# A long convolution by FFT in front of a token-mixing MLP: second forward stage in eight 64x32 tiles, first stage in units of four rows and half of the frequencies, shuffled as 448 KB to 16 partitions

## The chip, the core and the metric

The kernel runs on one core of one Trainium2 chip. The metric is device time in microseconds, the median of several executions. The engines that matter here are TensorE (PE; PEld is its weight load), VectorE (DVE), ScalarE (ACT), GpSimd (POOL) and SyncE (SP). GpSimd and SyncE also issue the DMAs that move data between partitions.

## The reference, cut to what matters

Everything has sequence length S = 2048 and D = 448 channels.

```python
def _A_ref(q, k, v, shift_k, ssm_k, ssm_D):
    # k_shift: causal convolution of k with 4 taps per channel
    for t in range(ks):
        k_shift = k_shift + k_pad[:, t:t + S, :] * shift_k[:, ks - 1 - t][None, None, :]
    kv = k_shift * v
    # causal convolution of kv with ssm_k (2048 taps per channel), by an FFT of length 2 S
    kv_f = rfft(kv padded to 2 S); kf_f = rfft(ssm_k padded to 2 S)
    y = irfft(kv_f * kf_f)[:, :S]
    y = y + kv * ssm_D[None, None, :]
    return q * y

def _B_ref(x, w1, b1, w2, b2):
    u = gelu(einsum("bsd,sf->bdf", layernorm(x), w1) + b1)      # F = 1792
    return transpose(einsum("bdf,fs->bds", u, w2) + b2)

h  = x + _A_ref(layernorm(x), k, v, shift_k, ssm_k, ssm_D)      # x is A_q
h2 = h + _B_ref(layernorm(h), w1, b1, w2, b2)
```

## The kernel before, in words

The FFT is written as matmuls with small tables, in two stages. It is done twice forward: for the filter ssm_k (tag "k", tensors KT and TK, steps k1 and k2) and for the product kv (tag "u", tensors V and TU, steps u1 and u2). A sequence position is 16 q + r, with q on 128 partitions and r = 0 to 15 in the free dimension.

**First stage** (`emit_stage1`, matmuls in L1040). For every r a table `E` (two variants x, 128 frequencies each) is multiplied with the data of row r. The matmuls are 128 x 32 column tiles: four rows r stand in the four column tiles, so four matmuls can run side by side. The loop takes four rows (`i`, four times) and in them a quarter of the frequencies (`jh`, four times). Such a group has eight matmuls into a pair of PSUM banks, and one eviction of 128 x 896 to a ring buffer `GR_`: by a copy on ScalarE or VectorE (L1050), or for the first four rows of k by a VectorE addition (L1048), which adds ssm_D on the way. There are 16 groups for each tag. The ring has four buffers of all four quarters (`gring`).

**Shuffle** (L1056). The second stage needs all 16 rows of a frequency together, so after every second group (a pair of quarters) three DMAs scatter the ring buffer to partitions in steps of four of T (TK or TU): two of 112 KB to 8 partitions each from POOL, one of 224 KB to 16 partitions from SP. A pair of quarters lands in half of T's 16 columns: columns with j mod 4 = 0 or 1 from the first pair, 2 or 3 from the second. T has the shape [16 columns, 2, 448] on 128 partitions.

**Second stage** (`emit_stage2`, matmuls in L1075). For each pair of columns `jj` (eight of them) and each half h there are four matmuls with the block table `FW`, 128 rows by 64 columns, two column tiles side by side; then one eviction of 128 x 896 for each h back into T (L719 to L723; for k with a scale, L720 on ScalarE and L723 on VectorE).

**Products and first inverse stage** (`emit_products_i1`). VectorE multiplies TU with TK (L1108), eight matmuls in 64 x 128 row tiles apply the inverse table (L1120), the result is evicted into TU (L719 or L722), and DMAs from POOL and SP scatter it to TZ (L1144; L1133 for the last columns). The second inverse stage (L1240) and the MLP (L1365, L1375, L1387) follow. The loads of w1 and w2 (L1338, L1342, L1349) are issued on SP once the last POOL scatter is done; the load of q (L896) waits for all shuffles of u.

**The convolution of k** with four taps (`emit_kv`) is done by transposes (L947), matmuls in 64 x 128 row tiles (L973) and a VectorE multiplication with v (L988). The first stage of u needs its output. The transposes of ssm_k (L1019), which the first stage of k needs, come before. `emit_tables` makes E, FW and the inverse tables from iotas on POOL (L773 to L787), VectorE integer operations (L803 to L847) and sines on ScalarE (L828, L843); `fields` holds the bit fields that are cut from the partition number. L1006 are matmuls without use that keep TensorE busy at the start.

**What sets the order.** Every operation is recorded with its reads and writes, and a list scheduler (`_Sched.schedule`) puts them in order at build time. Each step of a tag has a rank in the list `WHEN`; among the operations that are ready in the scheduler's own model, an engine takes the one with the lowest rank. `WHERE` says for each eviction whether ScalarE ("a"), VectorE ("d") or whichever is free ("f") takes it. Each engine then works through its list in order and waits where data are not there yet. PSUM has eight banks in four pairs; a group of first or second stage holds a pair until it is evicted.

Of the kernel before, what the change touches and what calls it, by code (L numbers as in the profile page):

```python
# [7 lines left out]
ALU = mybir.AluOpType  # L8
# [4 lines left out]
    "dummy": (283,),  # L13
    "tables": (138, 234, 288, 20, 81, 325, 139, 217,),
    "loads": (91, 107, 134, 143, 231, 216, 80, 297, 0, 238, 183, 285, 228, 299, 145,),
    "kv": (290, 148, 151, 174, 63, 282, 100, 192, 205, 47, 18, 112, 141, 45, 207, 160, 233,),
    "kT": (201, 13, 14, 175, 200, 130, 54, 53,),
    "k1": (132, 135, 152, 226, 122, 144, 165, 213, 68, 51, 154, 167, 89, 168, 262, 336,),
    "k2": (23, 150, 83, 97, 224, 227, 140, 153, 258, 248, 180, 195, 169, 219, 338, 235,),
    "u1": (71, 86, 116, 123, 46, 82, 176, 221, 117, 215, 261, 316, 173, 184, 277, 278,),  # L20
    "xload": (156, 298, 314, 302,),
    "bias": (75, 171,),
    "q": (271, 208, 318, 93, 268, 185, 279, 280, 264,),
    "u2": (133, 142, 220, 210, 241, 249, 64, 114, 159, 196, 137, 189, 1, 115, 252, 251,),
    "i1": (179, 121, 99, 3, 190, 96, 186, 149, 188, 240, 203, 202, 128, 92, 212, 95,),
    "ct": (36, 187, 87, 300,),
    "xn": (257, 17, 6, 222, 161, 317,),
    "w1a": (329, 239, 230, 55,),
    "w1b": (306,),
    "warm": (291, 307, 265, 27, 292, 147, 330, 320, 5, 304, 270, 38, 19, 315, 284, 62, 333, 327, 105, 118, 191, 295,  # L30
        324, 259, 56, 8, 332, 113, 236, 273, 206, 198, 182, 274,),
    "i2": (260, 69, 103, 39, 15, 31, 293, 28, 108, 242, 90, 84, 88, 331, 22, 197, 204, 33, 110, 237, 164, 323, 256,
        310, 73, 214, 223, 170, 44, 79, 157, 177, 16, 211, 328, 281, 131, 250, 4, 247, 158, 294, 109, 40, 29, 104,
        34, 243, 267, 129, 98, 287, 70, 178, 67, 162, 246, 120, 155, 2, 125, 11, 229, 42, 253, 272, 59, 124, 119,
        266, 12, 78, 194, 276, 127, 41, 313, 10, 102, 61, 255, 21, 37, 66, 24, 232, 199, 321, 312, 76, 308, 296, 52,
        111, 303, 163, 319, 58, 65, 339, 209, 26, 326, 337, 289, 85,),
    "w2": (146,),
    "mlp": (218, 57, 136, 126, 77, 30, 25, 48, 60, 9, 305, 72, 166, 245, 301, 172, 50, 181, 418, 419, 420, 421, 422,
        423, 424, 425, 426, 427, 428, 429, 430, 431, 432, 433, 434, 435, 436, 437, 438, 439,),
}  # L40
WHERE = {
    "kv": "ddaffffa",
    "kT": "fadfdddd",
    "k1": "fafaafaffaff",
    "k2": "dfdffadaafdafada",
    "u1": "fffaafadaaddafaa",
    "bias": "a",
    "u2": "fdaafafaaaaadafa",
    "i1": "affadfaaffdaffaf",
    "ct": "ffda",  # L50
    "xn": "aaff",
    "i2": "aaffaadafddf",
# [518 lines left out]
def _build(nc, A_q, A_k, A_v, A_shift_k, A_ssm_k, A_ssm_D, B_w1, B_b1, B_w2, B_b2, out):  # L571
# [5 lines left out]
    Bsz, S, D = A_q.shape  # L577
    F = B_w1.shape[1]
    assert Bsz == 1 and S == 2048 and D == 448 and F == 1792 and A_shift_k.shape[-1] == 4
    R = 16  # L580
    NFC = F // 128
    EPS = 1e-5
    DB = 2 * D
# [42 lines left out]
    with ctx:  # L626
# [47 lines left out]
        o_GR = (o_WR, o_WR + 8 * DB, o_X, o_X + 8 * DB)  # L674

        def GR_(s):
            return view(o_GR[s], [R // 4, 2, D])
# [13 lines left out]
        gring = _Pool(4)  # L691
# [36 lines left out]
        def emit_tables():  # L728
# [44 lines left out]
            op("pool", lambda e, W: e.iota(pc[:, 0:1], [[0, 1]], base=0, channel_multiplier=128), w=[(o_p, 4)])  # L773
            op("pool", lambda e, W: e.iota(gcol, [[0, 8], [512, 16]], base=0, channel_multiplier=0), w=[(o_gc, 512)],
               n=128, est=190.0)
            op("pool", lambda e, W: e.iota(chi, [[0, 2], [1, 4], [0, 16]], base=0, channel_multiplier=0),
               w=[(o_gc + 512, 512)], n=128, est=190.0)
            for a, b_, c_ in ((0, 112, 14), (112, 128, 2)):
                op("pool", lambda e, W, a=a, b_=b_, c_=c_: e.iota(gcm[:, a:b_], [[0, 8], [512, c_]], base=512 * 14 * (a > 0),
                                                                 channel_multiplier=0),  # L780
                   w=[(o_gc + 1536 + 4 * NB, 512, "gm")], n=128, est=190.0)
                op("pool", lambda e, W, a=a, b_=b_, c_=c_: e.iota(chm[:, a:b_], [[0, 2], [1, 4], [0, c_]], base=0,
                                                                 channel_multiplier=0),
                   w=[(o_gc + 2048 + 4 * NB, 512, "cm")], n=128, est=190.0)
            for k, (b0, st_) in enumerate(((2048, -2048), (2048, 2048), (0, 2048))):
                for a, b_ in (((0, 128),) if k == 0 else ((0, 112), (112, 128))):
                    op("pool", lambda e, W, k=k, b0=b0, st_=st_, a=a, b_=b_: e.iota(  # L787
                        cph[:, 128 * k + a:128 * k + b_], [[st_, 2], [0, (b_ - a) // 2]], base=b0, channel_multiplier=0),
                       w=[(o_gc + 1536 + 512 * k, 512, "cp%d" % k)], n=128, est=190.0)
# [7 lines left out]
            fields = ((5, 12), (0, 2048), (9, 3), (7, 15), (7, 15), (11, 3), (13, 1), (11, 2))  # L797
            o_fd = small(64)
            fd = view(o_fd, [16], i32)
            for i, (sh, mk) in enumerate(fields):  # L800
                op("pool", lambda e, W, i=i, sh=sh: e.memset(fd[:, i:i + 1], sh), w=[(o_fd + 4 * i, 4)], est=34.0)
                op("pool", lambda e, W, i=i, mk=mk: e.memset(fd[:, 8 + i:9 + i], mk), w=[(o_fd + 32 + 4 * i, 4)], est=34.0)
            op("dve", lambda e, W: e.tensor_tensor(out=pc[:, 4:12], in0=pc[:, 0:1].broadcast_to([128, 8]), in1=fd[:, 0:8],  # L803
                                                   op=ALU.logical_shift_right),
               r=[(o_p, 4), (o_fd, 32)], w=[(o_p + 16, 32)], n=8)
            op("dve", lambda e, W: e.tensor_tensor(out=pc[:, 4:12], in0=pc[:, 4:12], in1=fd[:, 8:16], op=ALU.bitwise_and),
               r=[(o_p + 16, 32), (o_fd + 32, 32)], w=[(o_p + 16, 32)], n=8)
            for i in (10, 11):
                op("dve", lambda e, W, i=i: e.tensor_tensor(out=pc[:, 4:5], in0=pc[:, 4:5], in1=pc[:, i:i + 1],
                                                            op=ALU.bitwise_or),  # L810
                   r=[(o_p + 16, 4), (o_p + 4 * i, 4)], w=[(o_p + 16, 4)], n=1)
# [218 lines left out]
        def emit_stage1(src, o_src, T, o_T, tag):  # L1030
            shuf[tag] = []
            for i in range(R // 4):
                g = _Buf(gring)
                for jh in range(4):
                    sch.t0 = T_K1 + T_DK1 * (4 * i + jh) if tag == "k" else T_U1 + T_DU1 * (4 * i + jh)
                    b = _Buf(psum, 2)
                    c0 = 64 * (jh & 1) + 32 * (jh >> 1)
                    for x in range(2):
                        for q, r in enumerate((4 * i, 4 * i + 2, 4 * i + 1, 4 * i + 3)):
# [5 lines left out]
                    def fn(e, W, b=b, g=g, jh=jh, i=i):  # L1045
                        dst = GR_(g.slots[0])[:, jh]
                        if tag == "k" and i == 0:
# [3 lines left out]
                    first = tag == "k" and i == 0  # L1051
                    op("dve" if first else FX, fn, r=[(o_DR, DB)] if first else [], br=[b], bw=[g], n=2 * D, kind="psum")
                    if jh % 2 == 0:
                        continue
                    for q_, a, nu in (("pool", 0, 8), ("pool", 96, 8), ("sp", 32, 16)):
                        shuf[tag].append(op(q_, lambda e, W, g=g, i=i, a=a, nu=nu, jh=jh: e.dma_start(  # L1056
                            T[a + i:a + i + 4 * nu - 3:4].rearrange("p (j k) c d -> p j k c d", k=4)[:, :, jh - 1:jh + 1]
                            .rearrange("p j k c d -> p j (k c d)"),
                            GR_(g.slots[0])[a:a + 4 * nu, jh - 1:jh + 1].rearrange("p k c d -> p (k c d)")),
                           br=[g], w=[(o_T + (4 * j + jh - 1) * 2 * DB, 4 * DB, tag) for j in range(4)],  # L1060
                           dmab=4 * nu * 4 * DB, keng=nu, rate=350.0))
# [5 lines left out]
        def emit_stage2(T, o_T, scale):  # L1067
            for jj in range(R // 2):
                bs = [_Buf(psum, 2) for _ in range(2)]
                for h in range(2):  # L1070
                    sch.t0 = (T_K2 if scale else T_U2) + T_D2 * (2 * jj + h)
                    for c in range(2):
                        for par in range(2):
                            j = 2 * jj + par
                            op("pe", lambda e, W, b=bs[h], h=h, j=j, c=c, par=par: e.matmul(  # L1075
                                PS[64 * par:64 * par + 64, b.slots[c], 0:D], FW[:, 64 * c:64 * c + 64], T[:, j, h, :],
                                start=True, stop=True),
                               r=r_fw + [(o_T + (2 * j + h) * DB, DB)], bw=[bs[h]], n=D, est=94.5, mode=2)
                for h in range(2):
                    i = 2 * jj + h  # L1080
# [17 lines left out]
        def emit_products_i1():  # L1098
            for jj in range(R // 2):
                ms = []  # L1100
                for h in range(2):
                    i = 2 * jj + h
                    sch.t0 = T_I1 + T_DI1 * i
# [12 lines left out]
                for h in range(2):  # L1116
                    for t, (tab, xy) in enumerate(((MA, 0), (MN, 3), (MB, 1), (MB, 2))):
                        for par in range(2):
# [5 lines left out]
                    evac(lambda jj=jj, h=h: TU[:, 2 * jj:2 * jj + 2, h, :], lambda b=bs[h]: Ppair(b),  # L1124
                         [(o_TU + (4 * jj + h) * DB, DB), (o_TU + (4 * jj + 2 + h) * DB, DB)], bs[h], 2 * D)
                if jj == R // 2 - 1:
                    for h in range(2):
                        for par in range(2):
                            j = 2 * jj + par
                            p0 = 64 * (j & 1) + 32 * ((j >> 1) & 1) + (j >> 2)  # L1130
# [9 lines left out]
                for par in range(2):  # L1140
                    j = 2 * jj + par
                    p0 = 64 * (j & 1) + 32 * ((j >> 1) & 1) + (j >> 2)
# [307 lines left out]
```

## Time and profile before

| what | value |
|---|---|
| median of 3 runs | 178.6 us (177.21 to 179.88) |
| the profiled execution | 178.13 us, its span 175.9 us, granted TensorE clock 1.0 |
| PE busy | 166.1 us (94%) |
| DVE, ACT, POOL busy | 102.0, 92.2, 63.3 us |
| first stage L1040 | 256 matmuls, 13.65 to 43.6 us |
| second stage L1075 | 128 matmuls, 35.99 to 67.2 us |
| first inverse stage L1120 | 128 matmuls, 53.59 to 73.3 us |
| shuffles L1056 | 32 issues on POOL (17.5 us), 16 on SP; 2.2 to 5.7 us from issue to landing, median 3.7 |
| MLP L1365, L1375, L1387 | from 85.59 us to the end |

How to read it: an engine row in a window is busy time, with the number of instructions in brackets. In a timeline, a line is a run of like instructions: start, length, engine, line of the kernel, shapes, number, and in square brackets how long the engine stood idle before it and what ended that. PE's busy time includes the pipeline of a matmul: one of 448 columns is shown with some 350 ns, though the next can start after 187.

### The profile page before, as it was taken

How to read it: one execution, taken by the hardware profiler on the slowest of the kernel's cores; microseconds unless marked ns; L12 is line 12 of the kernel's file. 1: busy time of each engine (PE TensorE's matmuls, PEld its weight loads, DVE VectorE, ACT ScalarE, POOL GpSimd, SP SyncE). 2: the span in 40 equal slices, each digit the busy share in tenths (PEclk: the TensorE clock that was granted, in tenths of full speed). 3: DMA queues.
4: the chain of work that ended last, by engine and by line, in shares of the span. 5: the costliest groups of instructions: out<-in, count | busy, mean ns of one | idle time of the engine just before them, and what ended most of it. 6: DMA issues, size and time to landing. Idle time of an engine off the chain costs nothing.

```text
span 175.9 us, 3619 instructions
## 1 busy us (share of the span) xinstructions
PE 166.1 (94%) x1445; PEld 95.6 (54%) x1445; DVE 102.0 (58%) x189; ACT 92.2 (52%) x131; POOL 63.3 (36%) x157
## 2 busy tenths in 40 slices
PE   6999999879979999998999999999999999999994
PEld 2786745342323333644544455555557777777784
DVE  6995696848999999998998860000001231331331
ACT  3799958888979999966982656412120000000000
POOL 8576628670600643894888760000000000000000
PEclk9999999999999999999999999999999999999999
DMA  5999855992849386569999999910000111011111
GB/s 174 416 334 332 268 165 201 325 352 71 250 98 383 110 214 198 167 179 390 383 396 405 421 419 417 419 77 0 0 4 0 52 52 52 16 40 52 52 52 52
DMA packets 15444, 35.13 MB, mean 200 GB/s; under 512 B 3820, under 2 KB 9484, under 8 KB 15428
## 3 DMA queue, kind: packets, MB, share of 16 engines
q1 hardware_dynamic: 12164, 28.00, 43.4%
q0 software_dynamic: 3072, 6.80, 12.6%
q8 instruction: 11, 0.18, 0.4%
q10 hardware_dynamic: 192, 0.11, 0.2%
q14 instruction: 5, 0.04, 0.1%
HBM read 22.05 MB, written 1.84 MB: 136 GB/s over the span
## 4 chain that ended last, share of the span: by engine, by line
PE 68%; ACT 10%; POOL 7%; DMA 7%; DVE 4%; issue 2%; DVEq 0%; POOLq 0%
PE ps L1387 24%; PE ps L1375 12%; PE ps L1365 9%; ACT arena L719 8%; DMA arena<-arena 7%; PE ps L1040 4%; PE ps L1006 3%; POOL arena L1056 3%; PE ps L947 3%; PE ps L1240 3%; PE ps L1075 2%; PE ps L1019 2%; PE ps L973 2%; PE ps L1120 2%; DVE arena L1259 1%
## 5 line engine op out<-in xcount | busy, mean ns | idle before, releaser
L1390 DVE SCALAR_TENSOR_TENSOR arena<-ps,arena 128x448 bf16<-128x448 f32 (+2 forms) x17 | 11.1, 656 | 57.4 <-PE ps L1387 57.4
L1387 PE MATMUL ps<-arena 128*128 128x448 bf16 (+2 forms) x238 | 42.7, 342 | 0.0
L1387 PEld LDWEIGHTS ps<-arena 128*128 128x128 bf16 x238 | 33.3, 145 | 9.5
L719 ACT CAST arena<-ps 128x896 bf16<-128x896 f32 (+1 forms) x29 | 23.4, 948 | 1.2 <-PE ps L1075 1.1
L1365 PE MATMUL ps<-arena 128*128 128x448 bf16 x112 | 22.9, 353 | 0.4 <-DVE arena L1318 0.4
L1056 POOL DMA_DIRECT2D arena<-arena x32 | 17.5, 553 | 14.1 <-ACT arena L1050 12.9
L1050 ACT CAST arena<-ps 128x896 bf16<-128x896 f32 x24 | 20.3, 919 | 3.8 <-PE ps L1040 3.5
L1375 PE MATMUL ps<-arena 128*128 128x448 bf16 x112 | 21.8, 353 | 0.0
L1075 PE MATMUL ps<-arena 128*64 128x448 bf16 x128 | 15.8, 360 | 3.4 <-DMA arena<-arena 1.8
L1355 ACT ACTIVATE arena<-ps,arena 128x448 bf16<-128x448 f32 x14 | 8.6, 633 | 19.4 <-PE ps L1375 17.7
L1108 DVE TENSOR_TENSOR arena<-arena 128x1792 bf16<-128x1792 bf16 x16 | 16.7, 1080 | 0.2
L1365 PEld LDWEIGHTS ps<-arena 128*128 128x128 bf16 x112 | 10.6, 98 | 11.5 <-DVE arena L1318 2.5
L1375 PEld LDWEIGHTS ps<-arena 128*128 128x128 bf16 x112 | 10.9, 98 | 10.2
L1040 PE MATMUL ps<-arena 128*32 128x448 bf16 x256 | 15.3, 356 | 0.4 <-DVE arena L988 0.3
L1120 PE MATMUL ps<-arena 64*128 64x448 bf16 x128 | 14.0, 352 | 1.0 <-ACT arena L719 0.9
L1144 POOL DMA_DIRECT2D arena<-arena x14 | 8.2, 588 | 17.4 <-ACT arena L719 16.6
L1075 PEld LDWEIGHTS ps<-arena 128*64 128x64 f16 x128 | 5.7, 108 | 12.8 <-ACT arena L719 3.6
L1287 ACT ACTIVATE arena<-arena 128x448 bf16<-128x448 f32 x14 | 8.0, 575 | 5.9 <-DVE arena L1259 5.7
L988 DVE TENSOR_TENSOR arena<-ps,arena 128x512 bf16<-128x512 f32 (+1 forms) x16 | 9.0, 617 | 2.7 <-PE ps L973 2.7
L1120 PEld LDWEIGHTS ps<-arena 64*128 64x128 f16 x128 | 5.1, 94 | 9.5 <-ACT arena L719 5.0
L719 ACT COPY arena<-ps 128x1024 bf16<-128x1024 bf16 (+1 forms) x9 | 8.9, 1019 | 0.9 <-PE ps L1154 0.6
L1040 PEld LDWEIGHTS ps<-arena 128*32 128x32 f16 x256 | 5.1, 95 | 7.8 <-DVE arena L988 1.9
(94 smaller groups left out, 207.0 us busy)
## 6 DMA issues: line engine op xcount, KB each, us to landing
arena<-in_B_w_dram SPq DMA_DIRECT2D x8, 896.0 KB, 12.0
arena<-in_B_w_dram SPq DMA_DIRECT2D x2, 2048.0 KB, 17.1
arena<-arena SPq DMA_DIRECT2D x16, 224.0 KB, 3.7
arena<-arena POOLq DMA_DIRECT2D x32, 112.0 KB, 3.8
arena<-in_B_w_dram SPq DMA_DIRECT2D x2, 1536.0 KB, 18.7
arena<-arena POOLq DMA_DIRECT2D x14, 196.0 KB, 4.6
arena<-in_A_k_dram SPq DMA_DIRECT2D x4, 448.0 KB, 5.7
arena<-in_A_v_dram SPq DMA_DIRECT2D x4, 448.0 KB, 9.0
```

Source lines behind the costliest of these rows:

```text
L719: return e.copy(out=dst(), in_=src())
L988: return e.tensor_tensor(out=v, in0=u.rearrange("p t (r d) -> p t r d", d=64), in1=v, op=ALU.mult)
L1040: op("pe", lambda e, W, b=b, r=r, q=q, x=x, c0=c0: e.matmul(PS[32 * q:32 * q + 32, b.slots[x], 0:D], E[:, 2 * r + x, c0:c0 + 32], src[:, r ...
L1050: return e.copy(out=dst, in_=Ppair(b)) if W == "act" else e.tensor_copy(out=dst, in_=Ppair(b))
L1056: shuf[tag].append(op(q_, lambda e, W, g=g, i=i, a=a, nu=nu, jh=jh: e.dma_start(T[a + i:a + i + 4 * nu - 3:4].rearrange("p (j k) c d -> p ...
L1075: op("pe", lambda e, W, b=bs[h], h=h, j=j, c=c, par=par: e.matmul(PS[64 * par:64 * par + 64, b.slots[c], 0:D], FW[:, 64 * c:64 * c + 64], ...
L1108: op("dve", lambda e, W, m=m, i=i: e.tensor_tensor(out=MR(m.slots[0]).rearrange("p (x y) d -> p x y d", x=2), in0=TU[:, i].unsqueeze(2).br ...
L1120: k = op("pe", lambda e, W, b=bs[h], m=ms[h], par=par, t=t, tab=tab, xy=xy, P=P: e.matmul(Pb(b, par), tab[P, :], MR(m.slots[0])[P, xy, :], ...
L1365: op("pe", lambda e, W, r=r, fc=fc, b=bs[fc]: e.matmul(Pb(b), W1A[:, r, 128 * fc:128 * fc + 128], Q[:, r, :], start=(r == 0), stop=(r == R ...
L1375: op("pe", lambda e, W, r=r, fc=fc, b=b: e.matmul(Pb(b), W1B[:, r, 128 * (fc - n0):128 * (fc - n0) + 128], Q[:, r, :], start=(r == 0), sto ...
L1387: op("pe", lambda e, W, r=r, fc=fc, b=b, d0=d0, d1=d1: e.matmul(Pb(b)[:, d0:d1], W2[fc // 7][:, fc % 7, r:S:R], G[:, fc, d0:d1], start=(fc ...
L1390: op("dve", lambda e, W, r=r, b=b, A=A, d0=d0, d1=d1: e.scalar_tensor_tensor(out=X[:, r, d0:d1], in0=Pb(b)[:, d0:d1], scalar=bm[:, r:r + 1 ...
```

## The change

The second stage takes 64 x 32 tiles: two halves t of the partitions, four column groups, eight matmuls that use different tiles. Per jj there are 16 matmuls in place of 8; its two columns are jj and jj + 8. So that each half of the partitions is a transform of its own, the first stage puts four rows and half of the frequencies (t) into one unit: a ring buffer holds two groups (`jh` = 0, 1), there are eight buffers of half the size, and each is scattered by one POOL DMA of 448 KB to 16 partitions in steps of four, p0 = 64 t + i4. It writes a part of all 16 columns of T. SP issues no shuffles any more. The tables, the bit fields and the scatter after the first inverse stage (p0) follow the new places. `WHEN` and `WHERE` have other values throughout: below are the rows that bear on the stages.

```diff
-    "loads": (91, 107, 134, 143, 231, 216, 80, 297, 0, 238, 183, 285, 228, 299, 145,),
-    "k1": (132, 135, 152, 226, 122, 144, 165, 213, 68, 51, 154, 167, 89, 168, 262, 336,),
-    "k2": (23, 150, 83, 97, 224, 227, 140, 153, 258, 248, 180, 195, 169, 219, 338, 235,),
-    "u1": (71, 86, 116, 123, 46, 82, 176, 221, 117, 215, 261, 316, 173, 184, 277, 278,),
-    "u2": (133, 142, 220, 210, 241, 249, 64, 114, 159, 196, 137, 189, 1, 115, 252, 251,),
+    "loads": (0, 146, 127, 221, 159, 158, 239, 300, 109, 296, 91, 316, 268, 277, 176,),
+    "k1": (139, 217, 15, 108, 34, 141, 120, 162, 175, 181, 105, 117, 107, 161, 137, 140,),
+    "k2": (218, 114, 168, 209, 164, 4, 232, 53, 206, 267, 69, 229, 61, 302, 270, 196,),
+    "u1": (182, 185, 226, 240, 68, 330, 73, 151, 269, 332, 208, 227, 215, 306, 210, 211,),
+    "u2": (36, 228, 272, 52, 143, 212, 282, 326, 122, 180, 262, 95, 238, 5, 111, 37,),
...
-        o_GR = (o_WR, o_WR + 8 * DB, o_X, o_X + 8 * DB)
+        o_GR = tuple(o + 4 * DB * s for o in (o_WR, o_X) for s in range(4))
...
-            return view(o_GR[s], [R // 4, 2, D])
+            return view(o_GR[s], [2, 2, D])
...
-        gring = _Pool(4)
+        gring = _Pool(8)
...
-            fields = ((5, 12), (0, 2048), (9, 3), (7, 15), (7, 15), (11, 3), (13, 1), (11, 2))
+            fields = ((6, 12), (0, 2048), (10, 1), (8, 15), (8, 15), (12, 3), (12, 3))
...
-            for i in (10, 11):
+            for i in (10,):
...
-            for i in range(R // 4):
+            for i in range(R // 2):
                 g = _Buf(gring)
-                for jh in range(4):
+                i4, t = i >> 1, i & 1
+                for jh in range(2):
...
-                    c0 = 64 * (jh & 1) + 32 * (jh >> 1)
                     for x in range(2):
-                        for q, r in enumerate((4 * i, 4 * i + 2, 4 * i + 1, 4 * i + 3)):
+                        c0 = 64 * (t ^ x) + 32 * jh
+                        for q in range(4):
+                            r = 4 * i4 + q
...
-                    if jh % 2 == 0:
-                        continue
-                    for q_, a, nu in (("pool", 0, 8), ("pool", 96, 8), ("sp", 32, 16)):
-                        shuf[tag].append(op(q_, lambda e, W, g=g, i=i, a=a, nu=nu, jh=jh: e.dma_start(
...
-                           br=[g], w=[(o_T + (4 * j + jh - 1) * 2 * DB, 4 * DB, tag) for j in range(4)],
-                           dmab=4 * nu * 4 * DB, keng=nu, rate=350.0))
+                p0 = 64 * t + i4
+                shuf[tag].append(op("pool", lambda e, W, g=g, p0=p0: e.dma_start(
+                    T[p0:p0 + 61:4].rearrange("p (j k) c d -> p j (k c d)", k=2),
+                    GR_(g.slots[0]).rearrange("p k c d -> p (k c d)")),
+                   br=[g], w=[(o_T, 32 * DB, tag)], dmab=128 * 4 * DB, rate=400.0))
...
             for jj in range(R // 2):
                 bs = [_Buf(psum, 2) for _ in range(2)]
+                for c in range(2):
+                    sch.t0 = (T_K2 if scale else T_U2) + T_D2 * (2 * jj + c)
+                    for h in range(2):
+                        for F_ in range(2):
+                            for t in range(2):
+                                j = jj + 8 * F_
+                                g0 = 64 * (t ^ h) + 32 * F_
+                                P = slice(64 * t, 64 * t + 64)
+                                op("pe", lambda e, W, b=bs[h], h=h, j=j, c=c, g0=g0, P=P, t=t: e.matmul(
+                                    PS[g0:g0 + 32, b.slots[c], 0:D], FW[P, 32 * c:32 * c + 32], T[P, j, h, :],
+                                    start=True, stop=True, tile_position=(64 * t, g0)),
+                                   r=r_fw + [(o_T + (2 * j + h) * DB, DB)], bw=[bs[h]], n=D, est=23.6, mode=5)
                 for h in range(2):
-                    sch.t0 = (T_K2 if scale else T_U2) + T_D2 * (2 * jj + h)
-                    for c in range(2):
-                        for par in range(2):
-                            j = 2 * jj + par
-                            op("pe", lambda e, W, b=bs[h], h=h, j=j, c=c, par=par: e.matmul(
-                                PS[64 * par:64 * par + 64, b.slots[c], 0:D], FW[:, 64 * c:64 * c + 64], T[:, j, h, :],
-                                start=True, stop=True),
-                               r=r_fw + [(o_T + (2 * j + h) * DB, DB)], bw=[bs[h]], n=D, est=94.5, mode=2)
-                for h in range(2):
-                    i = 2 * jj + h
+                    i = jj + 8 * h
...
-                    i = 2 * jj + h
-                    sch.t0 = T_I1 + T_DI1 * i
+                    i = jj + 8 * h
+                    sch.t0 = T_I1 + T_DI1 * (2 * jj + h)
...
-                    j = 2 * jj + par
-                    p0 = 64 * (j & 1) + 32 * ((j >> 1) & 1) + (j >> 2)
+                    j = jj + 8 * par
+                    p0 = 64 * par + 32 * (jj & 1) + (jj >> 1)
```

## The prediction

> **What bounds the kernel now.** I read the rows by stage first (forty slices, then windows of 10 us), then the chain that ended last, then the timeline of TensorE, ScalarE and VectorE between 13 and 52 us, where every edited line runs. From about 92 us on TensorE works through the MLP without a gap and nothing there is edited: a change can only move the moment at which that part begins. What counts is 13.65 us (first L1040) to about 73 us (last L1120).
>
> ```profile
> core 0: us, PE busy (x) PEld busy (x) DVE busy (x) ACT busy (x) POOL busy (x), PEclk, DMA share, GB/s
> 20.00:30.00 10.00, 9.73 (x221) 5.52 (x215) 8.68 (x13) 7.26 (x10) 4.77 (x10) 1.00 0.61 203
> 30.00:40.00 10.00, 8.30 (x151) 4.50 (x147) 6.47 (x9) 8.54 (x11) 6.86 (x13) 1.00 0.95 327
> 40.00:50.00 10.00, 9.39 (x104) 3.21 (x104) 9.16 (x12) 9.23 (x12) 3.24 (x6) 1.00 0.51 154
> 50.00:60.00 10.00, 8.55 (x80) 3.05 (x76) 9.84 (x10) 8.91 (x12) 2.13 (x4) 1.00 0.58 199
> 60.00:70.00 10.00, 9.30 (x82) 3.21 (x80) 9.72 (x15) 10.00 (x14) 3.71 (x7) 1.00 0.74 206
> ```
>
> The reader sees two regimes. From 50 to 70 us VectorE and ScalarE are full: second stage of u, products and first inverse stage are bound by evictions, and faster matmuls there are hidden. From 20 to 50 us ScalarE is idle 30 - 25.03 = 4.97 us and VectorE 5.69 us, together 10.7 engine-us or 5.3 us of time: the ceiling of what a better overlap can return.
>
> ```profile
> 32.20 2.35 PE L1040 MATMUL ps<-arena 128*32 128x448 bf16 x40
> 35.99 1.70 PE L1075 MATMUL ps<-arena 128*64 128x448 bf16 x16 [1.44 <-DMA arena<-arena]
> 37.95 0.95 PE L1075 MATMUL ps<-arena 128*64 128x448 bf16 x8 [0.25 <-ACT arena L720]
> 39.60 1.04 PE L1075 MATMUL ps<-arena 128*64 128x448 bf16 x8
> 40.57 3.02 PE L1040 MATMUL ps<-arena 128*32 128x448 bf16 x48
> 44.27 6.16 PE L1075 MATMUL ps<-arena 128*64 128x448 bf16 x48 [0.18 <-ACT arena L1050]
> 50.83 1.32 PE L1075 MATMUL ps<-arena 128*64 128x448 bf16 x12 [0.40 <-DMA arena<-arena]
> ```
>
> TensorE runs without a gap from 13.65 to 34.2 us, then waits for a shuffle. The second stage of k starts in halves: 16 + 8 + 8 = 32 of its 64 matmuls are done by 40.6 us, the four even jj, which need only columns of the first shuffle of each row group. Only then come the last six groups of u (L1040 x48), whose shuffles start late, so that u2 waits until 50.83.
>
> ```profile
> 36.53 2.19 POOL L1056 DMA_DIRECT2D arena<-arena  x4 [0.26 <-ACT arena L1050]
> 45.10 2.21 POOL L1056 DMA_DIRECT2D arena<-arena  x4 [0.33 <-DVE arena L1050]
> ```
>
> Four issues in a row: the last eviction of u ends at 45.03, the last issue at 46.77, and the data land at 50.79.
>
> **The change part by part.** Sums are made against the profiled execution (span 175.9, 178.13 us with 2.2 around it); the median is 178.6, and the difference found is taken off that.
>
> *Second stage, TensorE.* Today 128 matmuls of 128x64, two side by side. One pass of 448 columns takes about 187 ns (L1365 and L1375 run at 188 to 190 each), so a pair-wise one costs 94.5; sixteen in 1.70 us less the last one's own 0.35 confirm 90 to 96. After: 256 of 64x32, eight side by side, 23.4 each: 12.1 us become 6.0, 3.0 in k and 3.0 in u. No row has 64x32. Nearest: the convolution (L973, 64x128), where 24 instructions with 3072 columns, two side by side, take 0.77 us, 32 ns each, which is their streaming time (27 ns) and 5; and L1040 with four side by side, 53 ns where 46.7 would be ideal. Bounds: 23.4 ns and 53 ns (no gain). I take 24, since the weight loads of L1040 start in bursts of eight within 0.12 us and so do not hold the pace. The half in u is costed at nothing: the evictions of 50 to 70 us hide it; were that cover gone it would be worth up to 3.0 us. Only the start of u2 counts: ScalarE idles 1.09 us before 51.81, of which one jj takes 0.37 + 0.2 instead of 0.95: **-0.4**.
>
> The Trainium skill, "TensorEngine Tiling (Array Packing)", PSUM Bottleneck, speaks against this edit: tiling speeds TensorE up but not the emptying of PSUM, which may become the limit. The rows agree for k2 at 44 to 49 us (eight evictions without a pause); read strictly, the rule would leave -0.5 of this whole sum.
>
> *What cheap second-stage matmuls do before 34.5 us.* Between 20 and 34 us (windows of 2 us added up) ScalarE and VectorE idle 2.94 + 2.57 = 5.5 engine-us because TensorE is late, about 5.8 evictions at 0.95. If k2 is ready by then it can fill them: one eviction of it costs TensorE 4 x 94.5 = 0.38 us today, 0.19 after (a first-stage eviction costs 8 x 53 = 0.43). So 2.75 us of time are filled for 5.8 x 0.19 = 1.1: **-1.65**. Bounds: 0 (k2 not ready) and -2.75.
>
> *First stage.* 256 matmuls of 128x32 and 32 evictions stay, also the four VectorE additions of L1048. Nothing. The eight smaller ring buffers are freed after two evictions rather than four; no row of before shows a wait for a ring buffer, so nothing, at most -0.5.
>
> *Shuffles.* Removed: 32 POOL issues (553 ns) and 16 on SP. Added: 16 POOL issues with 128 rows of 3584 B; L1144 with 112 rows takes 588, so 0.59 each. POOL has 17.5 - 9.4 = 8.1 us less. SP keeps nothing between the loads and L896. On the path only the end counts: from 45.03 today 1.74 us to the last issue's end, after one issue 0.28 + 0.59: **-0.9** (bounds 0 and -1.7). Landing: the 48 of today take 2.2 to 5.7 us from issue, median 3.7. Each new one moves the 448 KB that three moved together; at the 377 GB/s of the busiest window the 336 KB beyond one POOL part cost 0.9 us if nothing ran beside it before and 0 if the parts overlapped: **+0.4**, bounds -1.8 and +1.7 (the extremes of landing against 4.02).
>
> The Trainium skill, "DMA: Bandwidth & Descriptors", gives about 2.0 us plus bytes at 436 GB/s for a GpSimd DMA: 3.05 for 448 KB. For 112 KB it would be 2.26 where the trace has 3.8, so the measurement decides; by the page the sum would be one microsecond better.
>
> *The wait that is added.* Each shuffle now writes a part of all sixteen columns, so every L1075 waits for all eight shuffles of its tensor; the start in halves is gone. Queued behind a waiting L1075 on TensorE are L1040 of u and the last convolution; ScalarE, VectorE, the u shuffles on POOL and then u2 wait for those. What covers it is the order. In the new priorities (lower first) fifteen of sixteen k1 steps stand at 15 to 181 and the last at 217, while thirteen of sixteen u1 steps stand below 270, and k2 cannot be placed before its data. So u1's last groups move ahead of k2's first eight evictions (5 on ScalarE, 3 on VectorE, about 4 us), and k2's sixteen evictions fill u1's shuffle time. From 34.5 to 48.9 us ScalarE works 13.2 and VectorE 11.6 us; evenly spread that is 12.4 of 14.4 us, so 2.0 are to be had; less the 0.6 until u2's first eviction, since its head start (four evictions, 48.9 to 51) is lost: **-1.4**. Bounds: -2.0 and, uncovered, +4.3 (second rival).
>
> *Tables and loads.* Two memsets (98 ns) and one L809 (144 ns) fewer, other iota patterns of the same number: nothing, hidden by the 20 us until FW is used. The load of the last ssm_k part now has 448 KB more ahead of it: at 416 GB/s 1.1 us. k1 began when the second sine table ended (13.03); its first rows now need only the first table. I take 0, bounds 0 and +1.1. Eviction strides in stage two and i1, and the scatter rows of L1144, keep count and size: nothing.
>
> Sum: -0.4 - 1.65 - 0.9 + 0.4 - 1.4 = -3.95, rounded to -3.9: **174.7 us**, 174.2 in the profiled execution's terms.
>
> **The rivals.**
>
> *Hidden anyway.* Evictions bind, k2 is not ready before 34 us, and only the shorter POOL tail and u2's start remain: -0.9 - 0.4 + 0.4 = -0.9, 177.7 us. For it: the pauseless evictions from 44 us on. Against: 10.7 engine-us idle before.
>
> *The barrier decides (the other side).* The last k1 group is a VectorE addition; today its L1048 ends at 35.55, its shuffles are issued from 36.53 and land at 36.53 + 3.8 = 40.3, and k2 ran 32 matmuls before that. If the last k1 step (rank 217) again comes among u1's, k2 starts 4.3 us later. It decides as soon as that landing is later than the last first-stage matmul that is ready. With u2's lost head start: 178.6 + 4.3 + 2.0 - 0.9 - 0.4 = 183.6 us. Against it: fifteen k1 steps come early.
>
> *Eight tiles do not run side by side.* At two, 256 x 94.5 = 24.2 us instead of 12.1; from 51 to 73 us TensorE would then need 12.1 + 14.0 = 26 us in 22, +4, and k2 +3 with half hidden: 178.6 + 4 + 1.5 = 184.1. At four, no gain, near the first rival. For it: no row shows this shape; against: the tiled shapes in the trace come within 20% of their ideal.
>
> **How the numbers follow.** Forecast 0.55, its own range 172.0 (all 5.3 us of idle time and the 1.3 of POOL tail and u2's start) to 176.5 (k2 not early); 0.46 of this lies below 175.0. Hidden 0.13, barrier 0.26, tiles 0.06. A measurement of this kernel tells about 2% (3.6 us) from no change: faster 0.46, same 0.09 + 0.13 = 0.22, slower 0.32. The range reaches up to the barrier's 183.6: 172.0 to 183.6.
>
> **What would show it.** Right: L1075's successor at 16 matmuls in about 0.55 us; k2 starting before 37 us and ending after the last first-stage matmul; u2's first matmul before 48 us; ScalarE and VectorE idle under 7 engine-us from 20 to 50; POOL issues near 0.6 us; the MLP's pauseless part beginning about 4 us earlier. Wrong: a TensorE wait for DMA above 2 us ahead of k2 or u2; landings above 6 us; 64x32 matmuls at 50 ns or more.

## The result, and the profile after

The kernel after takes **188.65 us** (median of 4 runs, 188.03 to 191.08); the kernel before, beside it, 177.99 us (177.21 to 179.88). The ratio is 1.0603, 95% interval 1.0521 to 1.0686: 10.7 us slower, outside the range of 172.0 to 183.6. The profiled execution took 188.42 us with a span of 186.6 us. Of the new lines, L1043 is the first stage, L1051 and L1053 its evictions, L1057 the shuffle, L1077 the second stage, L1122 the first inverse stage, L1146 its scatter, L1242 the second inverse stage. In the experiments the same lines stand a few lines lower: L1078 in e9 and e10 is the second stage, L1084 in e7, and L1147, L1243 and L1245 are the scatter and the second inverse stage of e9 and e10.

First the stages of the kernel after, in windows of 10 us:

```profile
core 0: us, PE busy (x) PEld busy (x) DVE busy (x) ACT busy (x) POOL busy (x), PEclk, DMA share, GB/s
20.00:30.00 10.00, 9.50 (x233) 6.00 (x225) 8.88 (x14) 6.59 (x9) 3.15 (x6) 1.00 0.92 204
30.00:40.00 10.00, 7.81 (x151) 3.11 (x151) 7.31 (x9) 6.53 (x8) 4.22 (x8) 1.00 1.02 217
40.00:50.00 10.00, 4.97 (x84) 1.50 (x88) 4.27 (x4) 5.69 (x7) 1.04 (x2) 0.52 1.02 218
50.00:60.00 10.00, 4.31 (x92) 1.16 (x80) 4.94 (x5) 4.88 (x7) 0.00 (x0) 0.67 0.66 159
60.00:70.00 10.00, 9.41 (x120) 3.09 (x112) 9.87 (x13) 10.00 (x13) 2.05 (x4) 0.95 0.46 169
```

Read the last two columns together. From 30 to 50 us the DMA engines are busy all the time (1.02) and move 217 GB/s. Before, they moved 327 GB/s at a *lower* share (0.95) between 30 and 40 us. The transfers are not more, they are slower. From 40 to 60 us every compute engine is idle about half of the time or more, and TensorE's clock falls to 0.52: the kernel waits.

TensorE's timeline shows for what:

```profile
37.03 1.37 PE L1043 MATMUL ps<-arena 128*32 128x448 bf16 x24 [0.15 <-ACT arena L1053]
44.41 1.70 PE L1077 MATMUL ps<-arena 64*32 64x448 bf16 x32 [6.01 <-DMA arena<-arena]
57.01 1.70 PE L1077 MATMUL ps<-arena 64*32 64x448 bf16 x32 [4.68 <-DMA arena<-arena]
```

The second stage of k begins at 44.41 us (before 35.99) after 6.01 us without work, that of u at 57.01 after 4.68. Together these waits are 10.7 us, where the two of before (1.44 and 0.40) were 1.8. The line of 50.83 us in the profile before isn't the start of u's second stage: four of its evictions ran from 48.9 us. ScalarE's first eviction of u, before and after:

```profile
48.90 1.82 ACT L719 CAST arena<-ps 128x896 bf16<-128x896 f32 x2
58.12 13.98 ACT L719 CAST arena<-ps 128x896 bf16<-128x896 f32 x17 [4.50 <-PE ps L1077]
```

It is 9.2 us later, the end of the first inverse stage 9.1 (82.4 against 73.3), the start of the second 10.3 (90.06 against 79.72). The last 1.2 us arise between the two inverse stages, where e9 loses time too (below). The chain of work that ended last names the transfers:

```profile
30.87 9.41 DMA arena<-arena
...
41.16 0.92 ACT arena L1053
...
42.37 0.52 POOL arena L1057
42.88 14.04 DMA arena<-arena
...
57.01 1.12 PE ps L1077 x16
```

Two shuffles of 448 KB, 9.41 and 14.04 us long. The first also holds a ring buffer: an eviction on ScalarE waited for it until 40.36 us, the next, at 41.16, stood behind that one, and its shuffle then landed last of all.

```profile
40.36 1.71 ACT L1053 CAST arena<-ps 128x896 bf16<-128x896 f32 x2 [2.57 <-DMA arena<-arena]
```

In the list of DMA issues the 16 shuffles read

```profile
arena<-arena POOLq DMA_DIRECT2D x16, 448.0 KB, 9.4
```

with 9.4 us as the median from issue to landing (4.5 to 15.0), where the 48 of before had 3.7. POOL is not what is late; its last two issues are on time behind their evictions:

```profile
37.55 1.06 POOL L1057 DMA_DIRECT2D arena<-arena  x2 [1.12 <-DVE arena L1053]
42.37 1.04 POOL L1057 DMA_DIRECT2D arena<-arena  x2 [3.76 <-ACT arena L1053]
```

16 x 448 KB are 7.34 MB; at 217 GB/s they need 33.8 us. Their packets run from 21.1 to 56.1 us, 35 us, which is 210 GB/s on average.

### The profile page after: what moved, and what is told of

Its sections match the earlier page's. It is cut to its first block, busy times and chain, and to the rows that moved or that the text cites. A ratio compares the mean times of both kernels' runs of the same rounds, so it can differ in the third digit from the quotient of the medians.

```text
span 186.6 us, 3819 instructions
## 1 busy us (share of the span) xinstructions
PE 165.0 (88%) x1573; PEld 93.8 (50%) x1573; DVE 102.6 (55%) x187; ACT 91.1 (49%) x132; POOL 53.9 (29%) x139
## 4 chain that ended last, share of the span: by engine, by line
PE 58%; DMA 15%; ACT 8%; POOL 7%; DVE 7%; issue 3%; DVEq 0%; POOLq 0%; ACTq 0%
PE ps L1389 23%; DMA arena<-arena 15%; PE ps L1377 11%; ACT arena L719 6%; PE ps L1122 5%; PE ps L1367 5%; PE ps L1007 3%; PE ps L1043 3%; PE ps L1020 3%; PE ps L974 3%; POOL arena L1313 2%; DVE arena L989 2%; PE ps L948 2%; POOL arena L1299 1%; DVE arena L1271 1%
## 5 line engine op out<-in xcount | busy, mean ns | idle before, releaser
L1077 PE MATMUL ps<-arena 64*32 64x448 bf16 x256 | 15.4, 477 | 12.8 <-DMA arena<-arena 10.7
L719 ACT CAST arena<-ps 128x896 bf16<-128x896 f32 (+1 forms) x28 | 22.8, 933 | 4.5 <-PE ps L1077 4.5
L1367 PE MATMUL ps<-arena 128*128 128x448 bf16 x112 | 22.7, 353 | 0.0
L1053 ACT CAST arena<-ps 128x896 bf16<-128x896 f32 x22 | 18.6, 911 | 8.4 <-PE ps L1043 5.7
L1377 PE MATMUL ps<-arena 128*128 128x448 bf16 x112 | 21.5, 352 | 0.0
L1146 POOL DMA_DIRECT2D arena<-arena x14 | 8.3, 596 | 30.7 <-ACT arena L719 29.7
L1377 PEld LDWEIGHTS ps<-arena 128*128 128x128 bf16 x112 | 11.0, 98 | 10.2
L1077 PEld LDWEIGHTS ps<-arena 64*32 64x32 f16 x256 | 4.0, 103 | 23.8 <-issue 12.6
L1043 PE MATMUL ps<-arena 128*32 128x448 bf16 x256 | 14.7, 355 | 0.7 <-ACT arena L1053 0.4
L1122 PE MATMUL ps<-arena 64*128 64x448 bf16 x128 | 13.8, 351 | 1.3 <-ACT arena L719 1.0
L1057 POOL DMA_DIRECT2D arena<-arena x16 | 8.7, 544 | 17.8 <-ACT arena L1053 13.2
L720 ACT ACTIVATE arena<-ps 128x896 bf16<-128x896 f32 x10 | 8.8, 920 | 4.6 <-PE ps L1077 4.6
L1122 PEld LDWEIGHTS ps<-arena 64*128 64x128 f16 x128 | 5.1, 94 | 9.7 <-ACT arena L719 5.4
L1242 PE MATMUL ps<-arena 128*128 128x448 bf16 x32 | 7.9, 353 | 2.1 <-DMA arena<-arena 1.5
L723 DVE TENSOR_SCALAR arena<-ps 128x896 bf16<-128x896 f32 x6 | 6.3, 1087 | 6.0 <-PE ps L1077 6.0
## 6 DMA issues: line engine op xcount, KB each, us to landing
arena<-in_B_w_dram SPq DMA_DIRECT2D x8, 896.0 KB, 13.2
```

Source lines behind the costliest of these rows:

```text
L719: return e.copy(out=dst(), in_=src())
L720: return e.activation(out=dst(), in_=src(), func=ACT.Copy, scale=scale)
L1043: op("pe", lambda e, W, b=b, r=r, q=q, x=x, c0=c0: e.matmul(PS[32 * q:32 * q + 32, b.slots[x], 0:D], E[:, 2 * r + x, c0:c0 + 32], src[:, r ...
L1053: return e.copy(out=dst, in_=Ppair(b)) if W == "act" else e.tensor_copy(out=dst, in_=Ppair(b))
L1077: op("pe", lambda e, W, b=bs[h], h=h, j=j, c=c, g0=g0, P=P, t=t: e.matmul(PS[g0:g0 + 32, b.slots[c], 0:D], FW[P, 32 * c:32 * c + 32], T[P, ...
L1122: k = op("pe", lambda e, W, b=bs[h], m=ms[h], par=par, t=t, tab=tab, xy=xy, P=P: e.matmul(Pb(b, par), tab[P, :], MR(m.slots[0])[P, xy, :], ...
```

## The experiments

**Theory:** the partitions that a shuffle writes limit its rate. Each new shuffle goes to 16 partitions in steps of four inside one half of the 128, and reaches only half of the ways into the memory. **Rivals:** the queue (one POOL queue now does what POOL and SP shared), the size of a transfer, and the added wait of the second stage for all eight shuffles. Unless the text says otherwise only the shuffles are edited; the order on every compute engine stays that of the kernel it comes from. In e1, e5, e6, e8, e9 and e10 the places are permuted against the tables, at the same bytes and counts.

### Places, number and queue

**e1_spread** makes two DMAs of each shuffle, one to each half of the partitions. **e2_split** is its control: the same two DMAs to the old places.

```diff
-    T[p0:p0 + 61:4] <- GR_                              # p0 = 64 * t + i4
+    T[64 * a + 32 * t + i4 : +29 : 4] <- GR_[64 * a:64 * a + 64]   for a in 0, 1     # e1_spread
+    T[64 * t + 32 * a + i4 : +29 : 4] <- GR_[64 * a:64 * a + 64]   for a in 0, 1     # e2_split
```

> The changed kernel with the order of every engine kept; each 448 KB shuffle is issued as two GpSimd DMAs of 224 KB to 8 partitions, one to partitions below 64 and one to partitions from 64 on (the places are permuted, so the output is not the reference's; all else is the same work). Theory 'half of the partitions': a shuffle that writes only into one half of the 128 partitions is held to about 217 GB/s, the rate of the saturated windows of the changed kernel, and the order keeps the shuffles of one half in front of the other's; spread over both halves the rate returns to 340 to 377 GB/s as before, landings fall from 9.4 us to 4 to 6, and the time to 176 to 181 us. Rival 'one GpSimd queue': the rate is that queue's, it stays at 205 to 230 GB/s and the time at 187 to 190 us. Rival 'barrier and order': the rate rises, but the time stays above 184 us.

> Control for the spread kernel: the same two DMAs of 224 KB to 8 partitions for each shuffle, the same order, but to the right places, so both write into one half of the partitions. Theory 'half of the partitions': as the changed kernel, 205 to 230 GB/s and 187 to 190 us. Rival 'size of the DMA' (448 KB in one piece is what is slow): as fast as the spread kernel. Rival 'one GpSimd queue': no change, 187 to 190 us.

Measured: e1 182.65 us (ratio 1.0200, 1.0119 to 1.0280), e2 188.53 (1.0518, 1.0437 to 1.0599). e1 stays above the 176 to 181 us that were expected and below the 184 of "barrier and order"; e2 is as the theory has it. The profiled executions took 186.42 and 191.81 us, each more than 3 us above its median. The windows from 32 to 40 us, of e1:

```profile
32.00:36.00 4.00, 3.80 (x84) 1.84 (x84) 3.21 (x5) 3.66 (x5) 3.21 (x7) 1.00 0.78 236
36.00:40.00 4.00, 3.85 (x84) 1.78 (x80) 3.42 (x6) 3.41 (x4) 2.11 (x5) 1.00 0.94 286
```

and of e2:

```profile
32.00:36.00 4.00, 3.75 (x80) 1.50 (x72) 3.21 (x5) 3.69 (x5) 2.13 (x5) 1.00 1.02 219
36.00:40.00 4.00, 2.86 (x48) 0.91 (x48) 2.53 (x5) 1.85 (x3) 1.75 (x4) 1.00 1.04 214
```

With the same 32 DMAs of 224 KB, the places alone make 236 to 286 GB/s of 214 to 219, and 5.9 us. Splitting a transfer without moving it changes nothing (188.53 against 188.65). The trace's records of single DMA packets say it more closely. A packet of 7168 bytes, the size in the shuffles that POOL issues, takes, in the median over the stretch of the shuffles:

| kernel | ns |
|---|---|
| before, e7, e9 | 276, 276, 273 |
| e1_spread | 272 |
| after, e2_split | 552, 520 |
| e3_two_queues, e5_step8 | 522, 540 |

In after the median packet takes twice as long, as if two of the 16 DMA engines shared one way in. In e1 it is back at the time of before. e1 doesn't reach the time of before all the same: in its profiled execution, the one of 186.42 us, the DMA engines have nothing to do for 6 to 22% of the time from 32 to 48 us (shares of 0.78 to 0.94), and k2 still waits 3.31 us. Why two half-sized DMAs from POOL fill the engines less well wasn't tried.

**e3_two_queues** issues every second shuffle (t = 1) on SP, **e4_all_sp** all of them.

```diff
-    op("pool", ... e.dma_start(T[p0:p0 + 61:4], GR_))
+    op("sp" if t else "pool", ...)      # e3_two_queues
+    op("sp", ...)                       # e4_all_sp
```

> The changed kernel with the order kept; the shuffles that write into partitions from 64 on are issued on SP, the others on GpSimd. Theory 'half of the partitions': where two shuffles for different halves are in flight the DMA engines take turns between the two queues and reach both halves at once, 300 GB/s and more in part of the windows; 179 to 185 us. Rival 'one GpSimd queue': half of the load leaves it, 177 to 182 us. Rival 'barrier and order': above 184 us.

> The changed kernel with the order kept; all sixteen shuffles are issued on SP and none on GpSimd. Theory 'half of the partitions': the queue is not the limit, 205 to 230 GB/s and 186 to 190 us. Rival 'one GpSimd queue': the rate goes to 300 GB/s and more, 177 to 182 us.

Measured: 187.07 us (1.0441, 1.0366 to 1.0516) and 187.44 (1.0483, 1.0424 to 1.0542); landings of 9.3 and 9.4 us in the median on either queue, and 202 to 227 GB/s from 28 to 44 us. The queue isn't the limit. e3 is slower than the 179 to 185 us that the theory had expected of it; its packet records give a hint why. Up to 44 us the transfers of the two queues mostly take turns, two to four microseconds of the one and then of the other, each packet at its slow pace. From 44 to 50 us packets of both queues run side by side, one half each: there those of 7168 bytes fall to 369 to 388 ns (medians over 2 us), and the windows of 2 us show 287 to 312 GB/s. That fits ways in that belong to each half.

### Is it the half, or the number of ways in?

**e5_step8** sends the 16 parts of a shuffle over all 128 partitions, in steps of eight.

```diff
-    T[p0:p0 + 61:4]        # 16 partitions, one half
+    T[i:i + 121:8]         # 16 partitions, both halves
```

> The changed kernel with nothing altered but the places of the shuffles: each still is one GpSimd DMA of 448 KB to 16 partitions, but in steps of eight over all 128 partitions rather than in steps of four over one half (the places are permuted against the tables; the work is the same). Theory 'half of the partitions', taken at its word: each shuffle now reaches both halves, so 300 GB/s and more, landings of 4 to 6 us, 178 to 184 us. Theory 'few ways in': what counts is how many separate ways into the memory a DMA's partitions have, and partitions in steps of eight have no more of them than partitions in steps of four over one half: 205 to 230 GB/s, landings near 9 us, 186 to 190 us. The Trainium skill, 'SBUF — State Buffer', Door 1: The DMA port swizzle, takes the second side: a port is chosen by bits 4 to 2 and bit 6 of the partition number, which makes 8 of 16 ports for either pattern.

Measured: 187.76 us (1.0525, 1.0476 to 1.0573), with landings of 8.7 us in the median, as "few ways in" has it.

```profile
32.00:36.00 4.00, 3.80 (x84) 1.65 (x80) 3.57 (x6) 3.40 (x5) 2.04 (x4) 1.00 1.01 230
36.00:40.00 4.00, 1.89 (x32) 0.45 (x32) 2.47 (x3) 1.75 (x3) 1.11 (x3) 1.00 1.03 235
```

Both halves are used and still 230 to 235 GB/s: "one half" was the wrong word. e9, further down, takes steps of four over both halves. The Trainium skill, "SBUF — State Buffer", Door 1: The DMA port swizzle, says which bits count: a partition's port is given by its bits 4 to 2 and bit 6, 16 ports in all. Steps of four in one half and steps of eight over all partitions both reach 8 of them. The page's rate for all 16 is 435 GB/s, half of which is 217. The windows of after and e5 show 204 to 235, within a tenth of that; no window of shuffles in these runs shows 435, the busiest 2 us of before are at 377.

### The kernel before with each part of the change

**e6_before_half** puts before's three DMAs of a unit into one half, in steps of two. **e7_before_barrier** lets its second stage wait for all 24 shuffles of a tensor. **e8_before_half_barrier** does both.

```diff
-    T[a + i:a + i + 4 * nu - 3:4]
+    T[64 * (i >> 1) + (i & 1) + a // 2 : +2 * nu - 1 : 2]          # e6, e8
...
+    for o_ in sch.ops:                                             # e7, e8
+        if o_.tag in ("k2", "u2") and o_.engs == ("pe",):
+            o_.late = shuf[o_.tag[0]]
```

> The kernel before with the order, the queues and the sizes of its 48 shuffles kept; only the places are permuted: the three DMAs of a unit write together into one half of the 128 partitions (32 partitions in steps of two) rather than over all 128 in steps of four. If the places alone slow the shuffles, the rate in the saturated windows between 28 and 40 us falls from 321 to 377 GB/s to 205 to 230, and the time rises to 181 to 186 us, with the waits of the second stage for DMA growing by some 3 us each. If 448 KB in one DMA, or GpSimd's queue, is what is slow, it stays at 177 to 180 us.

> The kernel before with the order of every engine kept; the matmuls of the second stage wait for all 24 shuffles of their tensor, as in the changed kernel, rather than for those of their columns. If the lost start in halves costs what the second rival of the prediction says (4.3 us at k2 and 2.0 at u2, less what follows can absorb), 181 to 185 us. If the order hides it, 178 to 180 us.

> Both alterations of the kernel before at once: places of the shuffles in one half of the partitions, and a second stage that waits for all shuffles of its tensor; the order of every engine kept. If these two are the changed kernel's loss, it shows about that loss, 186 to 191 us, though it has the old second stage and the old queues. If either hides the other, 183 to 186 us; if the new order or the 64x32 tiles cost time by themselves, it stays below 185 us.

Measured: e6 191.86 us (1.0739, 1.0678 to 1.0801), e7 188.68 (1.0572, 1.0516 to 1.0627), e8 205.70 (1.1509, 1.1444 to 1.1573). e6 is slower than expected, in rate (141 to 189 GB/s from 28 to 52 us, not 205 to 230) and in time (not 181 to 186 us); its profiled execution took 194.26 us. By the formula above one of its small DMAs reaches only four ports; no run tests whether that is the reason. e8 loses 27 us, more than e6 and e7 together (13.3 and 10.2) and than the 186 to 191 us expected; its k2 waits 19.10 us for shuffles. e7 is the surprise, far above the 181 to 185 us that were expected of a wait that costs:

```profile
41.74 3.83 PE L1084 MATMUL ps<-arena 128*64 128x448 bf16 x24 [6.77 <-DMA arena<-arena]
58.19 4.14 PE L1084 MATMUL ps<-arena 128*64 128x448 bf16 x24 [3.39 <-DMA arena<-arena]
```

With fast transfers (landings of 3.7 and 3.9 us) the full wait by itself costs 10.2 us *in the old order*. So by these runs alone the wait could explain the result as well as the places do. What decides is the wait with the new order and good places.

### The kernel after with good places alone

**e9_all32** sends each shuffle as one POOL DMA of 448 KB to 32 partitions in steps of four, over all 128. Number of DMAs, bytes, queue, order and the full wait stay.

```diff
-    T[p0:p0 + 61:4].rearrange("p (j k) c d -> p j (k c d)", k=2)
+    T[i4:i4 + 125:4].rearrange("p (j k) c d -> p j k c d", k=4)[:, :, 2 * t:2 * t + 2]
```

> The changed kernel with the order, the queue, the size and the number of its shuffles kept; each 448 KB DMA from GpSimd goes to 32 partitions in steps of four over all 128 (the pattern of the three DMAs of the kernel before taken together; the places are permuted against the tables), and the second stage still waits for all eight. If the places were all that the spread kernel lacked, the rate is 320 to 377 GB/s in busy windows, landings have a median of 4 to 5 us, and the time is that of the spread kernel or up to 4 us better, 178 to 183 us. What stays above 178 is then the wait for all shuffles together with the order in which the last unit of k comes late. If large GpSimd DMAs are slow by themselves, 185 to 189 us.

Measured: **177.80 us** (176.76 to 179.83, 10 runs), ratio 0.9960 (0.9910 to 1.0011), at the lower end of the 178 to 183 that were expected. In the windows:

```profile
32.00:36.00 4.00, 3.88 (x84) 1.64 (x76) 3.57 (x6) 3.69 (x5) 1.98 (x4) 1.00 0.91 318
36.00:40.00 4.00, 3.05 (x68) 0.97 (x70) 4.00 (x5) 3.76 (x5) 1.96 (x5) 1.00 1.01 363
```

and in TensorE's timeline:

```profile
38.10 0.57 PE L1078 MATMUL ps<-arena 64*32 64x448 bf16 x16
45.88 1.14 PE L1078 MATMUL ps<-arena 64*32 64x448 bf16 x32 [0.87 <-DMA arena<-arena]
```

363 GB/s, landings of 4.7 us in the median (3.0 to 5.9), no wait ahead of k2, 0.87 us ahead of u2. One line of addresses takes back all that was lost. It also doubles the partitions of a shuffle, but their number isn't what counts: e1 has the fast packet with 16 in all, and e6 is slow with 32 in one half. e9 also shows that the new order does cover the full wait, once transfers run at the higher rate.

### Where e9's head start goes

In e9 ScalarE's first eviction of u comes 2.2 us earlier than before (46.70 against 48.90), and the first inverse stage ends at 70.9 instead of 73.3.

```profile
46.70 9.00 ACT L719 CAST arena<-ps 128x896 bf16<-128x896 f32 x11 [0.41 <-PE ps L1078]
```

Yet the second inverse stage begins at 79.34 (before 79.72). The chain of e9:

```profile
72.73 0.65 POOL arena L1147
...
73.38 5.91 DMA arena<-arena
...
79.34 0.57 PE ps L1243 x2
```

In before the scatter that came last (L1133) was issued at 76.30 and took 3.37 us. In e9 the loads of the MLP's weights are issued on SP from 73.92 us, behind a scatter that is last in the text of the program but no longer in time. **e10_weights_wait** makes them wait for all scatters; **e9_again** is e9 beside it.

```diff
-    after=[shuf["zpool"]]
+    after=shuf["zall"]       # every scatter of the first inverse stage
```

> The kernel of e9_all32 once more, as the base for e10_weights_wait on the same chip. Expected 177.8 us, 0.99 to 1.00 of the kernel before.

> e9_all32 with one change: the loads of the MLP's weights on SP wait until all the scatters of the inverse's first stage have landed, and not only the one that is last in the program's text. The order on every engine is kept. In e9_all32 the weights were issued from 73.92 us, while the scatter that the inverse's second stage waits for was issued at 73.38 and took 5.91 us (3.37 before, where it was issued at 76.30 and the weights at 77.14). Theory 'the weights collide with the last scatter': it lands about 3.4 to 4.6 us after its issue, the inverse's second stage starts at 77.0 to 78.0 instead of 79.34, and the time is 175.4 to 176.6 us (0.98 to 0.99 of the kernel before). Rival 'the scatter takes that long by itself' (8 partitions, behind the other scatters): the second stage still starts at 79.0 to 79.6, and the time is 177.5 to 178.2. Third possibility: the second stage starts earlier but the weights come later by 3 us and the MLP waits for them: a wait for DMA before its first matmuls, time 177.5 or above.

Measured: e9 178.08 us (0.9966, 0.9933 to 0.9999), e10 **175.94** (0.9873, 0.9823 to 0.9922). The two intervals don't touch, and e10's time is the one that "the weights collide" expected. The chain of e9_again has

```profile
75.15 5.24 DMA arena<-arena
```

and in e10 the last scatter is issued at 75.46 too, TensorE's second inverse stage follows at 79.58, and the weights at 79.60:

```profile
79.58 2.44 PE L1245 MATMUL ps<-arena 128*128 128x448 bf16 x12 [0.47 <-DMA arena<-arena]
```

From issue to this start it is 4.1 us, with the DMA engines idle at the end, against 5.3 in e9_again (75.15 to 80.44), and TensorE's wait before it 0.47 against 1.64: the weights did hold this scatter up, and issuing them later costs the MLP less than it saves. But these two profiled executions differ by 1.25 us (178.85 and 177.60), the medians by 2.1, and e10's second inverse stage starts later than the 77 to 78 us that was expected, at the 79.0 to 79.6 of the rival. Its scatter takes 4 us without any weights beside it, and the execution runs some 2 us behind that of e9_all32 from its first stage on (16.96 against 14.92). How much of the 2.1 us is the collision stays open; the scatter itself shows 1.2.

## Why the prediction was wrong

**Landing of the shuffles: the step that failed.** It was put at +0.4 us with bounds of -1.8 and +1.7, from before's 377 GB/s and its landings of 2.2 to 5.7 us. The trace shows 9.4 us in the median and 14.04 for the one that counts. The rate was carried over from transfers that reach other partitions: a unit's three DMAs of before together cover 32 partitions in steps of four over all 128, each new one 16 in one half. The change states the new partitions in the open (p0 = 64 t + i4, steps of four), and the working never asked what they do to the rate. It named a page on the size of DMAs, where the page on the memory's ports was the one that bore on this. e9 undoes only this and measures 177.8: with the other terms left as they are, this one is worth 11.4 us by the ratios (1.0603 less 0.9960, times 178). An estimate from the 217 GB/s for half of the ports in the Trainium skill ("SBUF — State Buffer", Door 1) puts the landing of u's last shuffle 34 us after the first issue, at 53.5 us from after's 19.7; it came at 56.9.

**The ring buffers**, put at nothing, followed from it: a shuffle of 9.41 us held a buffer that an eviction of u waited for.

**The wait for all eight shuffles** was rightly listed, and its cover by the new order was right: 0.87 us in e9, with k2 starting straight behind the last first-stage matmul. Its price without that cover was put at +4.3, with u2's lost head start 6.3; e7 measures 10.2. The -1.4 for the new order's cover stands on busy times of 13.2 and 11.6 us from 34.5 to 48.9; the window itself has 12.9 and 11.3, which would make it -1.7. The rival "the barrier decides" had the right sign and the right symptom, a long TensorE wait for DMA ahead of k2, but at 183.6 us and for another reason.

**k2 as a filler before 34.5 us (-1.65)** was wrong as well, hidden under the large miss. Even with good places k2 starts at 38.10 us, since the last unit of k1 (rank 217) comes among those of u: its shuffle is issued at 34.00. The prediction's bound of 0 for this step was the value. Without it the sum is -0.4 - 0.9 + 0.4 - 1.4 = -2.3 us, and e10, which has good places and no collision at the end, lies 2.3 us under the kernel before (178.27 to 175.94). That the two agree is no proof of the single terms: e10 contains a change that the prediction didn't have.

**Eight tiles side by side** was right: 16 second-stage matmuls take 0.57 us in e9 (0.55 forecast), in two rounds of eight, the second 0.2 us after the first and 0.35 long; before's 16 took 1.70. The rival of two at a time is out. The issue on POOL was near too (0.53 to 0.55 us for 0.59).

**Of the signs named ahead,** landings above 6 us and a TensorE wait above 2 us for DMA were what would prove the forecast wrong, and both came. ScalarE and VectorE idle 20.7 engine-us from 20 to 50 us (10.7 before, 8.4 in e9), not under 7. One of the signs for it could not tell: "u2's first matmul before 48 us" already held before, at 47.89.

## What to carry to other kernels

Before two layouts are called equal in bytes, list the partitions that each DMA writes and ask which ways into the memory they reach; a transfer's rate in one layout is no bound for another. Here a share of 1.0 on the DMA engines at a rate well under that of another window meant that the destinations were the limit: another queue (187.07 and 187.44 us) and smaller transfers (188.53) gained little or nothing against 188.65. And where later work is ordered by "the last in the text", look whether it is still the last in time after a new order.

## What the runs showed of the hardware that was not expected

Neither the number of partitions nor that of transfers or queues set the rate: 16 partitions in steps of four in one half 204 to 225 GB/s, 16 in steps of eight over all 217 to 235, 32 in steps of four over all 318 to 363, steps of two in one half 141 to 189. The share of busy DMA engines was near 1.0 in all of these; the time of a packet told them apart, 272 to 276 ns against 520 to 552, and 660 for the POOL packets of e6.

In after TensorE's clock fell in the waits and stayed low behind them:

```profile
40.00:44.00 4.00, 0.00 (x0) 0.00 (x0) 1.09 (x1) 1.71 (x2) 1.04 (x2) 0.56 1.02 225
44.00:48.00 4.00, 3.14 (x60) 1.10 (x64) 2.09 (x2) 1.98 (x3) 0.00 (x0) 0.50 1.00 211
```

The granted clock is 0.56 from 40 to 44 us, within the 6 us without work, and 0.50 from 44 to 48, behind it. There 32 second-stage matmuls take 1.70 us, in e9 1.14. A wait of 1.44 us (before) and one of 2.31 us (e9, ahead of the second inverse stage) left the clock at 1.00; how long a wait it takes wasn't tried. The loss is small beside the waits: the first seven eighths of k2, 112 matmuls, span 7.9 us in after and 6.9 in e9.
